# Two attentions in one program: the first 1024 tokens of A transposed on TensorE, output weights through GpSimd's queue, the last 512 queries in two halves

## The chip, the cores and the metric

One core of one Trainium2 chip. The metric is the device time of one execution in microseconds (us), the median of several runs. "Before" is the kernel as it was, "after" the changed one. The span in the trace (first to last traced instruction) is 1.7 to 2.4 us shorter than the time of the same execution; both are named where they matter.

In the lines of the profile TensorE is PE (PEld its weight loads), VectorE DVE, ScalarE ACT, GpSimd POOL, SyncE SP; L752 is line 752 of that kernel. Lines in order of time begin with start in us and duration in us; in brackets is the idle time before it and what ended that. Apart from the 16 heads of attention, "head" is the start of the program. PSUM is the memory that TensorE writes its products to; the program deals it out in banks.

## The reference, cut to what matters

```python
# A: 2048 tokens, D = 448, 16 query heads of 28, ONE key/value head for all
q = (x @ wq).reshape(B, S, 16, 28);  k = x @ wk;  v = x @ wv
p = softmax(q k^T * 28**-0.5)             # full: 16 x 2048 x 2048
a = (p v) @ wo
# B: another x, 16 heads of 28, each position sees 8 earlier ones (steps of 2)
qkv = x @ wqkv
logits = q[s] . k[s - 2*w], w = 0..7      # masked below 0
b = softmax(logits) v[s - 2*w] @ wo
return concatenate([a, b], axis=-1)
```

A has 16 x 2048 x 2048 exponentials. In blocks of 128 keys by 512 queries that is 1024 score blocks. B has few exponentials, and fills gaps on TensorE and VectorE.

## The kernel before

The program is a list of operations, each with an engine, a modelled duration, reads, writes and a priority. A greedy list scheduler inside the program fixes the order on each engine before it is built; the built program has no choice left at run time. The modelled durations and priorities thus decide the order, and only the chip decides the times.

Loads (cut): the first 512 tokens of A come as they are and are transposed on TensorE. The rest come through transposing loads on SyncE's queue (SP). The output weights of A (`wo4`) and B (`wo_B`) come last, on the same queue.

```python
a("act", 0.5, load A_x[0:512] -> xst, W=["xst"], land=3.2, pr=-21)
a("act", 1.1, load wq, first part; gp: the other part)
for c in range(1, NCH):                   # chunks of 512 tokens, NCH = 4
    for t in range(4):
        a("sp", 1.05, transposing load of A_x chunk c -> xT_A, R=["xst"], ...)
for c in range(NCH):
    for t in range(4):
        a("sp", 1.05, transposing load of B_x chunk c -> xT_B, ...)
...
a("sp", 1.5, 4 loads -> wo_B, rel=4);  a("sp", 1.5, 4 loads -> wo4, rel=4)
```

Head: warm-up matmuls, the 16 transposes of chunk 0, K and Q of chunk 0, then the first scores. A further matmul on their squares (`q_sq` for Q, `d_u` for K, with `hq` as weights) completes each of them.

The loop over the score blocks: score slots of three and two PSUM banks in turn (`SLOTS`), one exponential on ScalarE (ACT) for each slot. In the rounds (one slot of three and one of two) that `OFF_AT` names, VectorE (DVE) takes the last bank of a three-bank slot and computes the exponential by a polynomial.

```python
SLOTS = ((0, 1, 2), (3, 4));  PVBANK = 5;  XBANKS = (6, 7);  TAILB = (0, 1, 2, 4);  WARM = 7
OFF_AT = {q: (0, 2, 5, 7) for q in range(1, 16)}            # quad q: 4 heads x 512 queries
OFF_AT.update({q: (0, 2, 3, 5, 7, 8) for q in (5, 9, 13)})
...
for i, (sc, t, tb, j) in enumerate(us):   # scores: 2 or 3 blocks on different row tiles
    matmul(bank(b0 + i), kT[32*j.., 128*tb..], qT[32*j.., sc % 2, t, :], tile_position=(32*j, 0))
a("act", t_exp(w), activation(expT, ps[:, 512*b0 : 512*b0 + w], Exp))
```

The end of a quad (`a_quad_end`): transpose the output product on VectorE, reciprocal, multiply, transpose again, then (every fourth quad) four output blocks through `wo4`. For the last quad this is done in two halves of columns, but both can begin only after the last exponential, since every output product covers all 512 queries.

B's work (`b_all`) is laid in by priorities that grow with `B0 = 22.0` and `BSTEP = 23.6`.

Of the kernel before, what the change touches and what calls it, by code (L numbers as in the profile page):

```python
# [12 lines left out]
D = 448  # L13
H = 16
DH = 28
# [15 lines left out]
TAILB = (0, 1, 2, 4)  # L31
WARM = 7
# [7 lines left out]
OFF_AT.update({q: (0, 2, 3, 5, 7, 8) for q in (5, 9, 13)})  # L40
# [53 lines left out]
class Sched:  # L94
# [49 lines left out]
    def run(self, engines):  # L144
# [44 lines left out]
        while left:  # L189
# [77 lines left out]
            if e == "pe":  # L267
                if o.use is not None and o.use.spare and o.alone and area(T) < (self.WANT if limit is None or T + o.dur + 0.18 <= limit + self.EPS else self.LOW):
                    o.fill = 1
                    o.dur += 0.18  # L270
                    o.dense += 512 - o.use.spare
                elif (o.full and area(T) < (self.FULL[o.full] if T + 0.22 * o.full + 0.2 <= H + self.EPS else self.LOW)
                      and all(d.start is not None and d.end + self.lat(d) <= T for d in o.opt)):
                    o.deps.update(o.opt)
                    o.dur = 0.22 * o.full
                    o.tiled = False
                    o.dense = 512 * o.full
                elif o.fill is not None:
                    o.full = 0
                    o.fill = max(0, min(0 if waiting else 2, round((self.WANT - area(T)) * self.WIN / 512 + 0.3)))  # L280
                    if T > 14 and area(T) > self.LOW:
                        o.fill = max(0, min(o.fill, int((H - 0.12 - self.MODE - T - o.dur + self.EPS) / 0.22)))
                    o.dur += 0.22 * o.fill
                    o.dense += 512 * o.fill
                if o.tiled and not mode:
                    o.dur += self.MODE
                mode = o.tiled
                if o.dense:
                    recent.append((T + o.dur, o.dense))
                    del recent[:-120]  # L290
# [108 lines left out]
class Gen:  # L399
# [63 lines left out]
    def alloc(self, es):  # L463
# [57 lines left out]
        self.xst = self.stage[:, 0:4 * D].rearrange("p (b c) -> p b c", c=D)  # L521
# [63 lines left out]
    def loads(self):  # L585
# [4 lines left out]
        def wload(dst, src, c0, c1):  # L590
# [4 lines left out]
            out=g.xst[:, :, :], in_=g.A_x[0, 0:512, :].rearrange("(b p) c -> p b c", p=128))),  # L595
          W=["xst"], dsem="i_xa0", land=3.2, pr=-21)
# [4 lines left out]
        for c in range(1, NCH):  # L601
            for t in range(4):
                a("sp", 1.05, one(lambda e, c=c, t=t: e.dma_start(
                    out=g.xT_A[:, t, 512 * c:512 * c + 512], in_=g.A_x[0, 512 * c:512 * c + 512, XB0[t]:XB0[t] + 128],
                    transpose=True)), R=["xst"], W=[("xT", c, t)], dsem=f"i_xa{c}.{t}", land=3.8, pr=-20 + c)
        for c in range(NCH):
            for t in range(4):
                a("sp", 1.05, one(lambda e, c=c, t=t: e.dma_start(
                    out=g.xT_B[:, t, 512 * c:512 * c + 512], in_=g.B_x[0, 512 * c:512 * c + 512, XB0[t]:XB0[t] + 128],
                    transpose=True)), W=[("xT_B", c, t)], dsem=f"i_xb{c}.{t}", land=4.5, pr=-16 + c)  # L610
# [8 lines left out]
        a("sp", 1.5, lambda e: [e.dma_start(  # L619
            out=g.wo_B[:, t, :], in_=bass.AP(g.B_wo.tensor, g.B_wo.offset + 7 * t * D, ap=[[D, 7], [DH * D, 16], [1, D]]))  # L620
            for t in range(4)], W=["wo_B"], dsem="i_wob", land=5, pr=2, rel=4, ninc=4)
        a("sp", 1.5, lambda e: [e.dma_start(
# [18 lines left out]
    def a_head(self):  # L641
# [6 lines left out]
        for c in range(NCH):  # L648
            pr = -9 if c == 0 else c
            HB = g.HB if c == 0 else g.LB  # L650
            for kt in range(4 if c == 0 else 0):
                u = Use(f"T{kt}", g.TB[kt:kt + 1])
                for b in range(4):
                    a("pe", 0.1, lambda e, u=u, kt=kt, b=b: e.transpose(  # L654
                        g.psb[:, 1024 * u.bank + 128 * b:1024 * u.bank + 128 * b + 128],
                        g.xst[:, b, XB0[kt]:XB0[kt] + 128], g.ident[:, :]),
                      R=["xst", "ident"], use=u, pr=-16, dense=128)
                dst = g.xT_A[:, kt, 0:512]
                src = lambda u=u: g.psb[:, 1024 * u.bank:1024 * u.bank + 512]
                if kt % 2:  # L660
                    a("dve", 0.42, lambda e, src=src, dst=dst: e.tensor_copy(out=dst, in_=src()), W=[("xT", 0, kt)], use=u, pr=-9)
                else:
                    a("act", t_act(512), lambda e, src=src, dst=dst: e.activation(dst, src(), ACT.Copy),
                      W=[("xT", 0, kt)], use=u, pr=-110)
# [27 lines left out]
            g.a_v(c)  # L692

# [65 lines left out]

    def a_loop(self):  # L760
# [4 lines left out]
        quads = {(sc, t): [[] for _ in range(4)] for sc in range(4) for t in range(4)}  # L765
# [6 lines left out]
        while pos < NU:  # L772
# [9 lines left out]
            def qk(e, us=us, b0=b0, box=[]):  # L782
                for _ in range(box[0].fill):
                    e.matmul(g.bank(b0), g.warm[:, 0:128], g.warm[:, :], start=True, stop=True)
                for i, (sc, t, tb, j) in enumerate(us):
                    if box[0].full:
                        r = e.matmul(g.bank(b0 + i), g.kz[:, j, 128 * tb:128 * tb + 128], g.qT[:, sc % 2, t, :], start=True, stop=True)  # L787
                        continue
                    r = e.matmul(g.bank(b0 + i), g.kT[32 * j:32 * j + 32, 128 * tb:128 * tb + 128],  # L789
                                 g.qT[32 * j:32 * j + 32, sc % 2, t, :], start=True, stop=True, tile_position=(32 * j, 0))  # L790
                return r
            box = []
            o = a("pe", 0.315, lambda e, qk=qk, box=box: qk(e, box=box), R=[("kT", tb // 4) for (_, _, tb, _) in us] + [("qT", sc % 2, t) for (sc, t, _, _) in us],
# [4 lines left out]
            o.opt = {x for (_, _, tb, _) in us for x in g.kz_ops[tb // 4]}  # L798
# [11 lines left out]
            for i in range(na):  # L810
                g.last_exp[b0 + i] = x
                quads[us[i][:2]][us[i][3]].append((us[i], ("expT", n % ERING), g.expT[:, n % ERING, 512 * i:512 * i + 512], 0))
# [5 lines left out]
            while late and late[0][0] <= n // 2:  # L818
                for x in late.pop(0)[1]:
                    qd = x[0][:2]  # L820
# [10 lines left out]
            for u in us:  # L831
                js = quads[u[:2]]
                while all(js):
                    g.pv_group([x.pop(0) for x in js])
                if u[2:] == (15, 3):
# [4 lines left out]
    def pv_group(self, grp):  # L840
        g, a = self, self.s.add
        qd = grp[0][0][:2]
# [3 lines left out]
        def pv(e):  # L846
            for (_, _, tb, j), _, src, w in grp:
                order = [o.seq for o, js in all_pv if j in js]
                first, last = box[0].seq == min(order), box[0].seq == max(order)
                x = e.matmul(g.bank(PVBANK, p0=32 * j, p1=32 * j + 32), g.v_aug[:, w, tb, :], src,  # L850
                             start=first, stop=last, tile_position=(0, 32 * j))
            return x
        o = a("pe", 0.315, pv, R=sorted({y[1] for y in grp}) + sorted(
            {(k, y[3], y[0][2] // 4) for k in ("v_aug", "v_aug1") for y in grp}), pr=-40, dense=700)
# [7 lines left out]
        if g.npv[qd] == 64:  # L862
            g.a_quad_end(*qd)

    def offload(self, n, us):

        g = self
        if n % 2 or us[0][:2] != us[-1][:2]:
            return 0
        if us[0][:2] != g.quad:  # L870
            g.quad, g.round = us[0][:2], n // 2
        return int(n // 2 - g.round in OFF_AT.get(4 * us[0][0] + us[0][1], ()))
# [28 lines left out]
    def a_quad_end(self, sc, t):  # L901
        g, a = self, self.s.add
        end = 12.0 + QT * (4 * sc + t + 1)
        last = sc == 3 and t == 3
        evacs = []
        hv = 2 if last else 1
        for hf in range(hv):
            w, b = 512 // hv, 16 // hv
            cs, bs = slice(w * hf, w * hf + w), slice(b * hf, b * hf + b)
            keys = [hf] if last else [0, 1]  # L910
            kk = lambda n: [(n, t % 2, x) for x in keys]
            p0 = -30 if last else -1
            o = a("dve", t_dve_ps(w), lambda e, cs=cs: e.transpose(out=g.PV_T[:, t % 2, cs], in_=g.bank(PVBANK)[:, cs]),  # L913
                  W=kk("PV"), pr=-30)
            o.deps.update(x for x, _ in g.pvs[sc, t])
            evacs.append(o)
            pt = g.PV_T[:, t % 2, :].rearrange("p (b e) -> p b e", e=32)
            a("dve", 0.25, lambda e, pt=pt, bs=bs: e.reciprocal(out=g.rden[:, t % 2, bs], in_=pt[:, bs, DH]),
              R=kk("PV"), W=kk("rden"), pr=p0)
            a("dve", t_dve_1x(w), lambda e, pt=pt, bs=bs: e.tensor_tensor(  # L920
                out=g.oN[:, bs, :], in0=pt[:, bs, :], in1=g.rden[:, t % 2, bs].unsqueeze(2).to_broadcast([128, b, 32]), op=ALU.mult),
              R=kk("PV") + kk("rden"), W=[("oN", x) for x in keys], pr=p0)
            a("dve", 0.12 + 1.04e-3 * w, lambda e, cs=cs: e.transpose(
                out=g.oTn[:, t, cs], in_=g.oN[:, :, :].rearrange("p b e -> p (b e)")[:, cs]),
              R=[("oN", x) for x in keys], W=[("oTn", t, x) for x in keys], pr=p0)
        g.evacs = evacs
        pr = end + 20
        if t < 3:
            return
        for s4 in range(4):  # L930
            blk = 4 * sc + s4
            if last:
                u = Use(f"F{sc}.{s4}", (TAILB[s4],), late=True)
            else:
                u = Use(f"F{sc}.{s4}", XBANKS)
            for tt in range(4):
                o = a("pe", t_mm(D), lambda e, u=u, s4=s4, tt=tt: e.matmul(  # L937
                    g.bank(u.bank, D), g.oTn[:, tt, 128 * s4:128 * s4 + 128], g.wo4[:, tt, :], start=tt == 0, stop=tt == 3),
                  R=[("oTn", tt, s4 // 2), "wo4"], W=[u], use=u, pr=pr + s4 + tt if not last else -30 + tt, dense=448)
                if last and tt == 0:  # L940
                    o.deps.add(g.last_exp[TAILB[s4]])
# [64 lines left out]
    def b_logits(self, k):  # L1006
# [4 lines left out]
        for t in range(4):  # L1011
# [9 lines left out]
            if k == 0:  # L1021
                op.deps.update(g.s.rd.get("xst", ()))
# [115 lines left out]
```

## Time and profile before

| what | before |
|---|---|
| time, median of 3 (range) | 460.67 us (460.61 to 460.84) |
| span of the profiled run | 459.2 us |
| start to first exponential ("head") | 11.29 us |
| first to last exponential ("stretch") | 440.43 us |
| last exponential to the end ("tail") | 7.47 us |
| blocks on ScalarE / VectorE | 958 / 66 |

The three pieces add up to the span. They come from one trace of each kernel. One more quantity is used, the **excess**: over all exponentials, the time from one start to the next instruction of ScalarE, less 0.8333 ns per column and 60 ns (the densest stretch of before keeps this rule: five exponentials of 13 blocks in 5.85 us). It sums the short stalls behind exponentials; before has 3.97 us. It leaves out the last exponential, and a wait that follows another instruction of ScalarE: 1.47 us in late_tr, 1.14 in old_head and in old_head_66, 1.30 in old_head_hold.

Two lines more of before that are needed later. The first is from the order of events (start in us, duration in us, then engine, line, operation, in brackets the idle time before it and what ended that), the second from the table of transfers, whose last number is the median time from issue to landing:

```profile
8.96 0.39 PE L752 MATMUL ps<-q_sq,hq 128*128 128x512 bf16 x1 [0.26 <-ACT q_sq L744]
...
xT_A<-in_A_x_dram SPq DMA_TRANSPOSE x12, 4.1
```

The matmul on `q_sq` starts as soon as ScalarE has the squares. From it to the first exponential are 11.29 - 8.96 = 2.33 us. A's twelve transposing loads land 4.1 us after their issue, at the median.

### The profile page before, as it was taken

To read this page: it belongs to the slowest core of one execution; us is meant where nothing else is said; L and a number is where in the kernel's file an instruction comes from. 1 tells how busy PE (TensorE), PEld (TensorE's weight loads), DVE (VectorE), ACT (ScalarE), POOL (GpSimd) and SP (SyncE) were. 2 spreads that over 40 slices of the span, in tenths; PEclk is the share of its full clock that TensorE was granted. 3 is DMA by queue.
4 is the path that set the end of the run, shared out by engine and by line. 5 is a ranking of instruction groups with operands and counts; after the bars stand their busy time and mean duration, and the time that the engine had idled before them with its cause. 6 is when DMAs were issued, how large, how long until landed. Compare 5 with 4: busy or idle time off the path is not lost.

```text
span 459.2 us, 8717 instructions
## 1 busy us (share of the span) xinstructions
PE 427.7 (93%) x3682; PEld 163.6 (36%) x3682; DVE 380.7 (83%) x622; ACT 444.9 (97%) x430; POOL 9.4 (2%) x29
## 2 busy tenths in 40 slices
PE   8999999999999989999899999899899998989997
PEld 3333232323533324234353342224244342325343
DVE  6556889988798898989688889998988969889883
ACT  3999999999999999999999999999999999999994
POOL 7000000000000000000000000000000000000000
PEclk9999999999999999999999999999999999999999
DMA  7774303002201002020220120002022221214001
GB/s 152 128 162 95 109 27 100 1 1 90 92 15 40 19 10 82 20 81 22 81 91 30 44 83 18 0 13 92 0 97 92 70 78 30 72 31 142 10 1 61
DMA packets 42102, 27.34 MB, mean 60 GB/s; under 512 B 17474, under 2 KB 41904, under 8 KB 42064
## 3 DMA queue, kind: packets, MB, share of 16 engines
q1 hardware_dynamic: 40464, 25.28, 19.6%
q0 software_dynamic: 304, 0.73, 0.6%
q10 hardware_dynamic: 1296, 0.79, 0.5%
q8 instruction: 29, 0.48, 0.4%
q14 instruction: 9, 0.07, 0.1%
HBM read 17.60 MB, written 5.52 MB: 50 GB/s over the span
## 4 chain that ended last, share of the span: by engine, by line
ACT 86%; PE 11%; DVE 1%; DMA 1%; issue 0%
ACT expT L806 85%; PE ps L789 2%; PE ps L1079 2%; PE ps L850 2%; PE ps L787 1%; DMA stage<-in_A_x_dram 1%; PE ps L978 1%; PE ps L1086 1%; PE ps L937 1%; ACT e_t L1054 0%; PE ps L654 0%; PE ps L738 0%; PE ps L1028 0%; PE ps L434 0%; PE ps L993 0%
## 5 line engine op out<-in xcount | busy, mean ns | idle before, releaser
L806 ACT ACTIVATE expT<-ps 128x1024 bf16<-128x1024 f32 (+1 forms) x410 | 438.8, 1209 | 2.1 <-PE ps L789 1.9
L789 PE MATMUL ps<-qT,kT 32*128 32x512 bf16 x824 | 122.3, 385 | 11.6 <-ACT expT L806 9.3
L850 PE MATMUL ps<-expT,v_aug 128*32 128x512 bf16 x958 | 94.8, 389 | 1.0 <-ACT expT L806 1.0
L787 PE MATMUL ps<-qT,kz 128*128 128x512 bf16 x200 | 59.6, 383 | 9.9 <-ACT expT L806 9.4
L789 PEld LDWEIGHTS ps<-qT,kT 32*128 32x128 bf16 x824 | 30.1, 91 | 91.7 <-ACT expT L806 68.4
L883 DVE TENSOR_SCALAR d_x<-ps 128x512 f32<-128x512 f32 x66 | 45.4, 688 | 17.9 <-PE ps L789 16.8
L850 PEld LDWEIGHTS ps<-expT,v_aug 128*32 128x32 bf16 x958 | 24.3, 93 | 62.0 <-issue 55.4
L1073 DVE TENSOR_TENSOR prod<-Vsh,a_n 128x896 bf16<-128x896 bf16 x64 | 37.5, 614 | 7.9 <-PE ps L1079 7.9
L1019 DVE TENSOR_TENSOR stage<-qTB,kTB 112x1024 bf16<-112x1024 bf16 x64 | 42.3, 674 | 1.8 <-PE ps L1028 1.7
L1079 PE MATMUL ps<-ident,prod 128*112 128x128 bf16 x512 | 41.8, 224 | 0.0
L894 DVE SCALAR_TENSOR_TENSOR d_u<-d_u,d_x 128x1024 f32<-128x1024 f32 x33 | 40.1, 1215 | 0.1
L896 DVE SCALAR_TENSOR_TENSOR dexp<-d_u,d_x 128x1024 int16<-128x1024 f32 x33 | 40.0, 1213 | 0.1
L892 DVE SCALAR_TENSOR_TENSOR d_u<-d_x 128x1024 f32<-128x1024 uint16 x33 | 39.9, 1209 | 0.2
L1079 PEld LDWEIGHTS ps<-ident,prod 128*112 128x112 bf16 x512 | 34.2, 130 | 14.7 <-issue 10.9
L978 PE MATMUL ps<-xT_B,wqkv 128*128 128x512 bf16 x128 | 38.9, 383 | 0.0
L787 PEld LDWEIGHTS ps<-qT,kz 128*128 128x128 bf16 x200 | 12.2, 97 | 31.1 <-ACT expT L806 28.9
L1028 PEld LDWEIGHTS ps<-ones,stage 112*128 112x128 bf16 x512 | 18.5, 96 | 7.8 <-issue 4.8
L1028 PE MATMUL ps<-ones,stage 112*128 112x4 bf16 x512 | 21.2, 167 | 0.0
L738 PE MATMUL ps<-xT_A,wq 128*128 128x512 bf16 x64 | 19.8, 384 | 0.1
L1086 PE MATMUL ps<-wo_B,oT 112*128 112x448 bf16 x64 | 18.1, 357 | 0.0
L993 PE MATMUL ps<-wqv,xT_B 128*128 128x448 bf16 x64 | 17.5, 356 | 0.0
L913 DVE STREAM_TRANSPOSE PV_T<-ps 128x512 f32<-128x512 f32 (+1 forms) x17 | 11.4, 676 | 6.7 <-PE ps L850 6.5
(103 smaller groups left out, 303.3 us busy)
## 6 DMA issues: line engine op xcount, KB each, us to landing
Vsh<-v_scratch SPq DMA_DIRECT2D x16, 896.0 KB, 4.6
v_scratch<-Vst SPq DMA_DIRECT2D x16, 112.0 KB, 1.7
out_dram<-outB SPq DMA_DIRECT2D x16, 112.0 KB, 1.7
out_dram<-outA SPq DMA_DIRECT2D x14, 112.0 KB, 1.7
wqkv<-in_B_wqkv_dram SPq DMA_DIRECT2D x1, 672.0 KB, 5.4
stage<-in_A_x_dram ACTq DMA_DIRECT2D x1, 448.0 KB, 4.0
wo_B<-in_B_wo_dram SPq DMA_DIRECT2D x4, 98.0 KB
wo<-in_A_wo_dram SPq DMA_DIRECT2D x4, 98.0 KB
```

The costliest lines, as they stand in the source:

```text
L787: r = e.matmul(g.bank(b0 + i), g.kz[:, j, 128 * tb:128 * tb + 128], g.qT[:, sc % 2, t, :], start=True, stop=True)
L789: r = e.matmul(g.bank(b0 + i), g.kT[32 * j:32 * j + 32, 128 * tb:128 * tb + 128], g.qT[32 * j:32 * j + 32, sc % 2, t, :], start=True, stop ...
L806: x = a("act", t_exp(w), lambda e, b0=b0, w=w, n=n: e.activation(g.expT[:, n % ERING, 0:w], g.ps[:, 512 * b0:512 * b0 + w], ACT.Exp, scale ...
L850: x = e.matmul(g.bank(PVBANK, p0=32 * j, p1=32 * j + 32), g.v_aug[:, w, tb, :], src, start=first, stop=last, tile_position=(0, 32 * j))
L883: o = a("dve", t_dve_ps(512), lambda e: e.tensor_scalar(out=xx[:, 512 * h:512 * h + 512], in0=g.bank(bank), scalar1=-128.0 * A2, scalar2=1 ...
L892: a("dve", t_dve_1x(1024), lambda e: e.scalar_tensor_tensor(out=u, in0=lo, scalar=EP * F, in1=lo, op0=ALU.add, op1=ALU.mult), R=di, W=["d_ ...
L894: a("dve", t_dve_1x(1024), lambda e: e.scalar_tensor_tensor(out=v, in0=u, scalar=EQ * F * F, in1=lo, op0=ALU.add, op1=ALU.mult), R=["d_u"] ...
L896: a("dve", t_dve_1x(1024), lambda e: e.scalar_tensor_tensor(out=out, in0=v, scalar=EL / F ** 3, in1=xx, op0=ALU.mult, op1=ALU.subtract), R ...
L978: a("pe", t_mm(512), lambda e, u=u, t=t, kt=kt, w=w: e.matmul(g.bank(u.bank), g.wqkv[:, kt, w * D + KC * t:w * D + KC * t + 128], g.xT_B[: ...
L1019: op = a("dve", t_dve_2x(1024), lambda e, t=t, qv=qv, kv=kv: e.tensor_tensor(out=g.prodT[0:KC, t, :, :], in0=qv, in1=kv, op=ALU.mult), R=R ...
L1028: r = e.matmul(g.bank(u.bank, 128).rearrange("p (h w) -> p h w", w=WIN)[:, 4 * t:4 * t + 4, w], g.prodT[0:KC, t, w, :], g.ones4[:, :], sta ...
L1079: a("pe", 0.056, lambda e, u=u, t=t, w=w: e.matmul(g.bank(u.bank, 128, 128 * t, p1=KC), g.prod2[:, w, KC * t:KC * t + KC], g.ident[:, :], ...
```

## The change

Its intent: a shorter tail, because the last 512 queries are done as two halves of 256, of which the first is finished before the last exponential; a second chunk of tokens that does not need the transposing loads; SyncE's queue relieved, so that B starts earlier; and a little less exponential work on VectorE, 62 blocks for 66.

The diff, cut to its core (left out: a modelled cost in the scheduler, by which scores that follow filling matmuls now take longer in its plan):

```diff
-TAILB = (0, 1, 2, 4)
-WARM = 7
+TAILB = (4, 0)
+WARM = 9
-OFF_AT.update({q: (0, 2, 3, 5, 7, 8) for q in (5, 9, 13)})
+OFF_AT.update({q: (0, 2, 3, 5, 7, 8) for q in (7,)})
+OFF_AT[15] = (0, 2, 3, 5)                       # and only in its first half
 # loads
+a("act", 0.5, load A_x[512:1024] -> xst[:, 4:8], W=[("xst", 1)], land=4.5, pr=-19)
-for c in range(1, NCH):   a("sp", 1.05, transposing loads of A, R=["xst"])
+for c in range(2, NCH):   a("sp", 1.3,  transposing loads of A, R=[("xst", 0)])
-                          a("sp", 1.05, transposing loads of B)
+                          a("sp", 1.3,  transposing loads of B)
-a("sp", 1.5, wo_B);  a("sp", 1.5, wo4)
+a("gp", 4, wo_B);    a("gp", 4, wo4)
 # head
-if c == 0: transposes on TensorE
+if c < 2:  g.a_tr(c)                             # chunk 1 too: two banks, four DVE copies
 # last quad
+def parts(self, u):                              # one block = two key blocks x 256 queries
+    if u[:2] == (3, 3):
+        return [(2 * (u[2] % 8) + i, 256 * (u[2] // 8), 256) for i in range(2)]
+    return [(u[2], 0, 512)]
-for i, (sc, t, tb, j) in enumerate(us): one matmul of 512
+for i, u in enumerate(us):
+    for k, (tb, q0, nq) in enumerate(g.parts(u)): one matmul of nq columns
-if g.npv[qd] == 64: a_quad_end(sc, t)            # both halves at the end
+if g.npv[qd] == (64 if len(qd) == 2 else 32): a_quad_end(sc, t[, half])
```

## The prediction

> **What bounds the kernel now.** I read the page's busy shares first, then who makes ScalarE wait, then the chain that ended last, then the first 12 and the last 20 us in order of time. ScalarE (ACT) is busy 97% of the span, and the chain goes through it:
>
> ```profile
> PE 427.7 (93%) x3682; PEld 163.6 (36%) x3682; DVE 380.7 (83%) x622; ACT 444.9 (97%) x430; POOL 9.4 (2%) x29
> ACT 86%; PE 11%; DVE 1%; DMA 1%; issue 0%
> ACT outA L944 <- PE ps L937: 3.4, 1, 3.4
> ACT expT L806 <- PE ps L789: 1.9, 1, 1.9
> ```
>
> Those two waits stand at the two ends: 1.9 us before the first exponential, 3.4 us after the last. Between them no wait is charged to ACT. So the time is three pieces: a head until the first exponential at 11.29, a stretch of exponentials until 434.81 + 16.91 = 451.72, and a tail until 459.2, that is 7.48 us. The stretch is 440.43 us. The groups by shape give what it is made of:
>
> ```profile
> L806 ACT ACTIVATE expT<-ps 128x1024 bf16<-128x1024 f32 x270 | 269.7, 1066 | 0.1
> L806 ACT ACTIVATE expT<-ps 128x1536 bf16<-128x1536 f32 x139 | 207.2, 1490 | 2.0 <-PE ps L789 1.9
> L806 ACT ACTIVATE expT<-ps 128x512 bf16<-128x512 f32 x1 | 0.8, 761 | 0.0
> L883 DVE TENSOR_SCALAR d_x<-ps 128x512 f32<-128x512 f32 x66 | 45.4, 688 | 17.9 <-PE ps L789 16.8
> ```
>
> There are 1024 score blocks of 128x512. VectorE (DVE) does 66 of them (L883), ACT the other 958 = 2x270 + 3x139 + 1. One block costs ACT 1490 - 1066 = 0.424 us; the number of instructions (410, two for every five blocks) does not depend on who does the block.
>
> The head, in order of time: load, transposes, K and Q, first exponential.
>
> ```profile
> 0.81 4.02 DMA stage<-in_A_x_dram
> 4.88 1.89 PE ps L654 x16
> 8.31 0.60 ACT q_sq L744
> 10.14 0.67 DVE kT L684
> 11.29 5.97 ACT expT L806 x5
> ```
>
> The tail, the same way (VectorE, then the last issue of SyncE):
>
> ```profile
> 452.41 0.78 DVE L913 STREAM_TRANSPOSE PV_T<-ps 128x256 f32<-128x256 f32 x2 [5.22 <-PE ps L850]
> 453.99 0.76 DVE L923 STREAM_TRANSPOSE oTn<-oN 128x256 bf16<-128x256 bf16 x2
> 454.67 0.65 DVE L1082 CAST oT<-ps 112x512 bf16<-112x512 f32 x1
> 455.25 1.14 DVE L947 CAST outA<-ps 128x448 bf16<-128x448 f32 x2
> 456.35 0.62 DVE L1089 CAST outB<-ps 128x448 bf16<-128x448 f32 x1
> 457.00 0.33 SPq L1091 DMA_DIRECT2D out_dram<-outB  x1
> ```
>
> The tail is not A's alone: B's last block (L1082, L1089) sits between A's steps on DVE, and its store is the last one issued.
>
> **What the Trainium skill says.** "ScalarE: Activation LUTs", What ACT_TABLE_LOAD costs, gives 186 ns + 0.833 ns per column for an ACTIVATE with immediates, and an overlap of about 93 ns back to back. That is 1039 ns for 1024 columns and 1466 for 1536; the trace has 1066 and 1490, within 3%, and its 0.424 us for 512 columns is the 0.427 of the page. "TensorE: Matmul & The Clock Gate", Part 1, gives 426.7 ns for 512 columns while PE is cold, 215.7 when warm, and about 3.4 us of activity in a free-running window to get there. The trace agrees on the pitches: seven warm-up matmuls take 3.17 us, sixteen transposes 1.89 (0.107 apart, so still cold), the four Q matmuls at 7.24 take 1.03, so warm. "TensorEngine Tiling (Array Packing)", Key Properties, lets different tiles work in parallel; the three scores of L789 take 0.39 us together, as much as one alone (mean 385 ns). "DMA: Bandwidth & Descriptors", Issuing engines are not separate DMA queues, says that another issuer only saves the sequencer's time; that is SyncE's 3.37 + 1.79 us for wo_B and wo at 41 to 46 us here.
>
> **The change part by part.**
>
> Fewer blocks on DVE. Before: twelve quads with 4 and three (5, 9, 13) with 6, 48 + 18 = 66. After: thirteen of quads 1 to 14 with 4, quad 7 with 6, and quad 15 with 4 in its first half only: 52 + 6 + 4 = 62. ACT gets four blocks back: 4 x 0.424 = +1.70 us, all on the path, since ACT has no idle time to take them. DVE loses 4 x 0.688 + 2 x (1.209 + 1.215 + 1.213) = 10.0 us, on an engine that doesn't bound.
>
> Stalls between exponentials. The densest stretch, 11.29 to 17.14, has five for 13 blocks in 5.85 us: 13 x 0.427 + 5 x 0.06. By that rule 958 blocks and 410 instructions take 433.4 us; eight L1054 cost some 0.31 each (89.06 to 89.37) and four gcol 0.06, 436.1 in all. The stretch is 440.4, so some 4 us are short stalls, mostly (my reading) where DVE must empty a third bank. Four of 66 such rounds fewer: -0.25.
>
> Last quad in halves. Each score is now two matmuls of 256 columns, issued one after the other on the same row tile before the next tile's, so three blocks take four steps of 0.107 us instead of two: about 0.21 us longer. After the exponential of a three-bank slot ACT has 0.91 us of the other slot to cover a 0.39 us score group; at 0.6 us this still fits if PE is prompt, and PE is not always. I put +0.3 over the 13 rounds. The output product alternates over four tiles, so its length stays 0.39.
>
> Head. The first 512 tokens take the same path as before. A second 448 KB load is put on ACT's queue behind the first and behind wq, so the first should land near 4.83. Nine warm-up matmuls instead of seven end near 1.25 + 9 x 0.427 = 5.1 instead of 4.2, 0.2 us after that landing; against it, the clock may be granted earlier. The second chunk's 16 transposes and four copies (4 x 0.42 us of DVE) must fit the idle gaps between 8.3 and 10.8; a copy ahead of L756 would cost up to 0.4. I put +0.2. SyncE sends 8 transposing loads of A (1.26 us each) instead of 12, so wqkv goes out 5 us earlier than 22.5 and B starts earlier. That doesn't move the stretch: in the head ACT shows no wait for keys even now. B's loads carried no hold on x in the diff's old side either; they only stand behind fewer of A's.
>
> GpSimd issues wo_B and wo: eight issues of 0.55 to 0.9 us, about 6 us from 10.2, done before its first v_aug copy at 17.4. Off the path: 0.
>
> Tail. From the last exponential to PV_T stays 0.69. With one half left, the VectorE chain is 0.43 + 0.18 + 0.40 + 0.42 (256-column means of L913, L918, L920, L923) and three hand-overs of 0.06 = 1.61, against 454.48 - 452.41 = 2.07. Then a matmul 0.06 + 0.2 later for the second block, its result 0.39 on, an ACT copy of 0.54 and a hand-over of 0.03; the store and the closing barrier, 459.2 - 457.0 = 2.2. Sum: 0.69 + 1.61 + 0.26 + 0.39 + 0.57 + 2.2 = 5.7 against 7.48, so -1.75. It needs B's last block out of the way: B starts 5 us earlier and DVE has 10 us less, so it should be done near 445.
>
> Sum: +1.70 - 0.25 + 0.3 + 0.2 - 1.75 = +0.2.
>
> **The rivals.** First, the tail gains nothing, because B's last block still ends last or the second half's output products wait for the first half (they share one bank, and the first half's DVE exponentials are ready late). For: in the trace B's blocks run some 40 us behind the times that the code sets. Against: DVE is busy only 6.4 of the last 11.7 us before the last exponential. Then about 462.5. Second, the halves or the head cost more: score groups late in each of 13 rounds by 0.2, or PE waiting in order for the second load before K and Q. For: PE is 93% busy. Against: PE waits for ACT 97 us in 242 waits. Then 463 to 464. Third, a better gain: the warm clock comes before the transposes (16 at 0.056 instead of 0.107, limited by the copies to some 0.5 us), and lighter quads 5, 9 and 13 remove more stalls than counted, 1 us. Then 458.5.
>
> **Range and chances.** +0.2 gives 460.9; I shade it to 460.6, since less on DVE and an earlier B can only shorten stalls. The range 458.4 to 463.0 holds the tail gain from none to full and either head. A change of 2% is 9.2 us, more than head stalls and tail together could lose without a new wait inside the stretch: 0.96 within, 0.02 each side.
>
> **What would show it.** L883 x62, ACT with 143 instructions of 1536 columns and 266 of 1024, and a stretch 1.3 to 2 us longer; the first exponential between 10.9 and 11.8; last exponential to end 5.5 to 6.2 us, with no L1089 after L947 and a store of A as the last one. Wrong would be: new waits of ACT for L789 or its successor inside the stretch, a first exponential after 12, a B store last, or a stretch not longer at all (then the stalls went with the four blocks).

## The result, and the profile after

| what | before | after |
|---|---|---|
| time, median (range, runs) | 460.71 us (460.58 to 461.08, 6) | 460.76 us (460.52 to 462.23, 6) |
| span of the profiled run | 459.2 | 458.8 |
| head | 11.29 | 12.02 |
| stretch | 440.43 | 441.01 |
| tail | 7.47 | 5.76 |
| blocks on ScalarE / VectorE | 958 / 66 | 962 / 62 |
| excess | 3.97 | 3.03 |

The ratio of the times is 1.0006, with a 95% interval of 0.9993 to 1.002: the same. A ratio here is always the mean time of one kernel's fast runs over that of the other's of the same rounds, so it is not quite the ratio of the medians that are quoted.

The page of after, its busy line and its chain of work that ended last:

```profile
PE 427.7 (93%) x3818; PEld 165.8 (36%) x3818; DVE 373.9 (81%) x617; ACT 445.3 (97%) x429; POOL 14.6 (3%) x37
...
ACT 93%; PE 4%; DMA 1%; DVE 1%; ACTq 0%; issue 0%
```

ScalarE's waits in after (total us, times, longest), the two that count:

```profile
ACT outA L968 <- PE ps L961: 2.8, 1, 2.8
ACT expT L832 <- PE ps L815: 2.2, 1, 2.2
```

ScalarE still bounds. Its two long waits are still only those at the ends: the tail's is shorter (2.8 for 3.4), the head's longer (2.2 for 1.9). VectorE has become less busy and TensorE is unchanged.

The groups by shape (count, then busy us and mean ns of one, then idle time before them):

```profile
L832 ACT ACTIVATE expT<-ps 128x1024 bf16<-128x1024 f32 x266 | 267.7, 1077 | 0.1
L832 ACT ACTIVATE expT<-ps 128x1536 bf16<-128x1536 f32 x143 | 214.0, 1497 | 2.2 <-PE ps L815 2.2
...
L911 DVE TENSOR_SCALAR d_x<-ps 128x512 f32<-128x512 f32 x62 | 42.6, 687 | 20.3 <-PE ps L815 19.4 <-PE ps L812 0.6
```

The counts are those that were predicted: 143, 266 and 62.

The head of after in order of time (TensorE, and the first exponential on ScalarE):

```profile
7.48 1.04 PE L751 MATMUL ps<-xT_A,wq 128*128 128x512 bf16 x4 [0.36 <-DVE wq L636]
9.47 0.40 PE L693 MATMUL ps<-ident,stage 128*128 128x128 bf16 x4 [0.31 <-DMA stage<-in_A_x_dram]
9.71 0.38 PE L765 MATMUL ps<-q_sq,hq 128*128 128x512 bf16 x1
12.03 1.45 ACT L832 ACTIVATE expT<-ps 128x1536 bf16<-128x1536 f32 x1 [2.23 <-PE ps L815]
```

L693 is a transpose of the second chunk. TensorE stood at it until the second load had landed, and the `q_sq` matmul (L765, L752 of before) had to wait behind it, although its squares were ready at 9.15 (8.55 + 0.60). It starts at 9.71 instead of 8.96. From it to the first exponential is 2.32 us, as before. So all of the +0.73 in the head passes through this one place in TensorE's order. A part of it is older: Q (L751) begins at 7.48 instead of 7.24, since VectorE's copy of wq began at 7.11 instead of 6.48. That leaves some 0.5 us for the wait behind the transposes. Two of the nine warm-up matmuls of the program came to stand behind the first sixteen transposes (at 6.30 and 6.73), so the first transposes began at 4.87, as before (4.88).

The tail of after (TensorE, VectorE, ScalarE and the two issuing queues, in order of time):

```profile
448.49 4.55 ACT L832 ACTIVATE expT<-ps 128x1536 bf16<-128x1536 f32 x4
...
453.54 0.45 DVE L938 STREAM_TRANSPOSE PV_T<-ps 128x256 f32<-128x256 f32 x1 [5.45 <-PE ps L878]
...
454.72 0.45 DVE L947 STREAM_TRANSPOSE oTn<-oN 128x256 bf16<-128x256 bf16 x1
...
455.23 0.55 PE L961 MATMUL ps<-wo,oTn 128*128 128x448 bf16 x2 [1.44 <-DVE oTn L947]
455.63 0.62 DVE L971 CAST outA<-ps 128x448 bf16<-128x448 f32 x1 [0.46 <-PE ps L961]
455.82 0.54 ACT L968 ACTIVATE outA<-ps 128x448 bf16<-128x448 f32 x1 [2.78 <-PE ps L961]
...
456.39 0.36 ACTq L973 DMA_DIRECT2D out_dram<-outA  x1
```

One half's chain, no work of B in it, and a store of A is the last one. B's last cast had been at 430.06 (456.35 before), although B had not started earlier: its first matmul on the tokens begins at 38.6 us (38.0 before).

The halves hardly slowed the score groups. Six matmuls of 256 columns take as long as three of 512 (0.39 us before). The ends of matmuls are modelled in a trace, but the semaphores agree: a group of six tells ScalarE 0.434 us after its first start, a group of three 0.415.

```profile
428.94 0.40 PE L815 MATMUL ps<-qT,kT 32*128 32x256 bf16 x6
```

Where the time went, in spans: head +0.73, stretch +0.58, tail -1.71, in all -0.40. The stretch is +1.71 for four more blocks (4 x 0.427), -0.94 of excess, and -0.17 in the last exponential, which the excess leaves out. Outside the span after takes 2.04 to 2.13 us in all its six runs, before 1.71 to 1.81 in most of its runs (and 2.2 to 2.35 in some): about +0.35. This cancels the -0.40 nearly.

### The profile page after: what moved, and what is told of

The parts are those of the page before. It is cut to its first block, busy times and chain, and to the rows that moved or that the text cites. A ratio compares the mean times of both kernels' runs of the same rounds, so it can differ in the third digit from the quotient of the medians.

```text
span 458.8 us, 8985 instructions
## 1 busy us (share of the span) xinstructions
PE 427.7 (93%) x3818; PEld 165.8 (36%) x3818; DVE 373.9 (81%) x617; ACT 445.3 (97%) x429; POOL 14.6 (3%) x37
## 4 chain that ended last, share of the span: by engine, by line
ACT 93%; PE 4%; DMA 1%; DVE 1%; ACTq 0%; issue 0%
ACT expT L832 92%; DMA stage<-in_A_x_dram 1%; PE ps L1103 1%; PE ps L815 1%; PE ps L812 1%; PE ps L878 1%; ACT e_t L1078 1%; PE ps L961 0%; ACTq L594 0%; PE ps L1052 0%; DVE qT L769 0%; DVE kT L676 0%; ACTq L593 0%; ACT outA L968 0%; ACTq L595 0%
## 5 line engine op out<-in xcount | busy, mean ns | idle before, releaser
L815 PE MATMUL ps<-qT,kT 32*128 32x512 bf16 (+1 forms) x859 | 120.8, 373 | 10.9 <-ACT expT L832 8.2
L878 PE MATMUL ps<-expT,v_aug 128*32 128x512 bf16 (+1 forms) x1022 | 95.2, 376 | 0.2 <-ACT expT L832 0.2
L812 PE MATMUL ps<-qT,kz 128*128 128x512 bf16 (+1 forms) x229 | 62.0, 363 | 9.6 <-ACT expT L832 9.1
L911 DVE TENSOR_SCALAR d_x<-ps 128x512 f32<-128x512 f32 x62 | 42.6, 687 | 20.3 <-PE ps L815 19.4
L1103 PE MATMUL ps<-ident,prod 128*112 128x128 bf16 x512 | 43.5, 224 | 0.1
L922 DVE SCALAR_TENSOR_TENSOR d_u<-d_u,d_x 128x1024 f32<-128x1024 f32 x31 | 37.6, 1214 | 0.2
L924 DVE SCALAR_TENSOR_TENSOR dexp<-d_u,d_x 128x1024 int16<-128x1024 f32 x31 | 37.6, 1213 | 0.1
L920 DVE SCALAR_TENSOR_TENSOR d_u<-d_x 128x1024 f32<-128x1024 uint16 x31 | 37.5, 1210 | 0.1
L812 PEld LDWEIGHTS ps<-qT,kz 128*128 128x128 bf16 x229 | 15.0, 97 | 29.5 <-ACT expT L832 27.4
L751 PE MATMUL ps<-xT_A,wq 128*128 128x512 bf16 x64 | 20.0, 384 | 0.7 <-DVE wq L636 0.4
L961 PE MATMUL ps<-wo,oTn 128*128 128x448 bf16 x64 | 16.8, 356 | 1.4 <-DVE oTn L947 1.4
```

The costliest lines, as they stand in the source:

```text
L812: r = e.matmul(g.bank(b0 + i, nq, nq * k), g.kz[:, j, 128 * tb:128 * tb + 128], g.qT[:, sc % 2, t, q0:q0 + nq], start=True, stop=True)
L815: r = e.matmul(g.bank(b0 + i, nq, nq * k), g.kT[32 * j:32 * j + 32, 128 * tb:128 * tb + 128], g.qT[32 * j:32 * j + 32, sc % 2, t, q0:q0 + ...
L878: x = e.matmul(g.bank(PVBANK, nq, q0, p0=32 * j, p1=32 * j + 32), g.v_aug[:, w, tb, :], src[:, nq * k:nq * k + nq], start=first, stop=last ...
L911: o = a("dve", t_dve_ps(512), lambda e: e.tensor_scalar(out=xx[:, 512 * h:512 * h + 512], in0=g.bank(bank), scalar1=-128.0 * A2, scalar2=1 ...
L920: a("dve", t_dve_1x(1024), lambda e: e.scalar_tensor_tensor(out=u, in0=lo, scalar=EP * F, in1=lo, op0=ALU.add, op1=ALU.mult), R=di, W=["d_ ...
L922: a("dve", t_dve_1x(1024), lambda e: e.scalar_tensor_tensor(out=v, in0=u, scalar=EQ * F * F, in1=lo, op0=ALU.add, op1=ALU.mult), R=["d_u"] ...
```

## The experiments

Twelve kernels ran. In the table, ratio is to the kernel before in the same rounds; before had medians of 460.89, 460.59, 460.85 and 461.0 us in the four batches (first four, next four, next three, last).

Each edit makes the scheduler lay a new order on all engines, so a run changes more on the chip than its edit says. And the first exponential moves from trace to trace, with the landing of the loads: 10.63 to 11.40 us in the nine traces with the old head, 11.47 to 12.63 in the four with the new one (late_tr apart).

| run | median us (range, runs) | ratio [95%] | head | stretch | tail | excess | ACT/DVE blocks |
|---|---|---|---|---|---|---|---|
| blocks66 | 462.37 (461.9 to 463.31, 6) | 1.0029 [1.0014, 1.0044] | 12.63 | 439.98 | 7.82 | 3.60 | 958/66 |
| late_tr | 462.10 (461.61 to 462.38, 6) | 1.0019 [1.0005, 1.0033] | 11.22 | 442.55 | 5.77 | 3.07 | 962/62 |
| old_head | 465.45 (463.52 to 468.64, 6) | 1.0095 [1.0065, 1.0125] | 10.96 | 447.29 | 5.78 | 8.22 | 962/62 |
| old_head_66 | 465.34 (464.68 to 467.71, 6) | 1.0103 [1.0078, 1.0128] | 10.63 | 444.26 | 8.50 | 6.65 | 958/66 |
| tail_only62 | 460.29 (460.14 to 461.33, 5) | 0.9996 [0.9983, 1.0008] | 10.92 | 441.35 | 5.96 | 3.17 | 962/62 |
| tail_only66 | 462.87 (462.53 to 462.95, 4) | 1.0045 [1.003, 1.006] | 11.40 | 440.18 | 9.33 | 3.62 | 958/66 |
| old_head_hold | 463.25 (463.04 to 464.84, 4) | 1.0063 [1.0049, 1.0078] | 10.96 | 444.95 | 6.97 | 5.62 | 962/62 |
| after_sp | 461.13 (461.03 to 461.46, 4) | 1.0011 [0.9997, 1.0025] | 11.64 | 441.51 | 5.96 | 3.13 | 962/62 |
| gp_only | 463.43 (462.33 to 463.92, 4) | 1.0046 [1.0031, 1.0061] | 11.16 | 443.44 | 7.47 | 7.16 | 958/66 |
| early66 | 458.25 (458.04 to 458.55, 5) | 0.9943 [0.9931, 0.9956] | 10.92 | 439.38 | 6.31 | 2.86 | 958/66 |
| mix64 | 458.64 (458.33 to 459.58, 5) | 0.9953 [0.9941, 0.9966] | 10.99 | 439.77 | 5.94 | 2.55 | 960/64 |
| early66_new_head | 461.67 (461.63 to 461.67, 5) | 1.0015 [1.0001, 1.0028] | 11.47 | 439.51 | 8.62 | 3.05 | 958/66 |

### What the four blocks bought: blocks66

```diff
 # after, but
-OFF_AT.update({q: (0, 2, 3, 5, 7, 8) for q in (7,)})
+OFF_AT.update({q: (0, 2, 3, 5, 7, 8) for q in (5, 9, 13)})
```

> The changed kernel with six DVE blocks in quads 5, 9 and 13 again and four in quad 7, so 66 DVE blocks instead of 62. Theory (a block costs ACT 0.427 us and brings back some 0.06 to 0.25 us of stalls): stretch 441.0 - 1.7 + 0.6 = 439.9 or less, time 459.7 or less. Rival (the three heavy quads are what stalled ACT before: excess over the dense rule was 4.0 us before and 3.0 after): stretch 440.7 to 441, excess back to 4, time 460.4 to 460.8.

Measured: 462.37 us, later than either expectation. The stretch fell by 1.03 us, but the tail grew by 2.06 (and the head by 0.60, since its loads landed later). The end of blocks66 in order of time:

```profile
455.75 0.69 DVE L1106 CAST oT<-ps 112x512 bf16<-112x512 f32 x1 [0.35 <-PE ps L1103]
456.36 1.15 DVE L971 CAST outA<-ps 128x448 bf16<-128x448 f32 x2
...
457.65 0.62 DVE L1113 CAST outB<-ps 128x448 bf16<-128x448 f32 x1
458.30 0.33 SPq L1115 DMA_DIRECT2D out_dram<-outB  x1
```

B's last block (L1106, L1113) is back in the tail and its store is the last one issued, as in the kernel before. With this head and these places the short tail came only with the four blocks taken from VectorE; the +1.71 and the -1.71 of the change then belong together. Whether the amount of work or its order decides is tested further below.

### What the head cost: late_tr

```diff
 # after, but the second chunk's transposes come after the first scores
-  W=[("xst", 1)], dsem="i_xa1", land=4.5, pr=-19)
+  W=[("xst", 1)], dsem="i_xa1", land=8.5, pr=-19)
```

The number is the modelled landing time. It changes no transfer, only the place of the transposes in TensorE's order.

> The changed kernel, but the schedule takes the second load of x to land 8.5 us after issue instead of 4.5, so that its 16 transposes stand behind the first scores in PE's order and no longer before L765. Theory (PE stood still for that load with the q_sq matmul behind it): the matmul after q_sq starts at 9.2 instead of 9.71, first exponential near 11.5 instead of 12.02, time near 460.3. Rival (L765 is late because Q was late, wq having landed later): first exponential 11.9 to 12.1, time unchanged at 460.8.

Measured: the head fell to 11.22, and another wait took its place. From the order of events of late_tr:

```profile
8.89 0.39 PE L765 MATMUL ps<-q_sq,hq 128*128 128x512 bf16 x1
...
11.32 0.95 PE L693 MATMUL ps<-ident,stage 128*128 128x128 bf16 x14
...
19.65 2.37 ACT L832 ACTIVATE expT<-ps 128x1536 bf16<-128x1536 f32 x2 [1.47 <-PE ps L815]
```

L765 does not wait for the load any more: it starts 1.72 us after Q (7.17), as in before, where after took 2.23. So the wait of some 0.5 us is shown. But now the keys of the second chunk come late, and ScalarE stalls 1.47 us before the exponential at 19.65. The median rose to 462.10 (against before the intervals of late_tr and after overlap). So the early place costs about 0.5 us and the late one about 1.5.

The rest of the +0.73 is Q's later start, and this goes with the second load too, but late_tr does not test it: the last part of wq that Q needs landed between 6.21 and 6.51 us in the nine traces without this load, and between 6.49 and 7.69 in the five with it (7.09 in after, 6.76 in late_tr).

In after, after_sp, blocks66 and early66_new_head the first transpose of the second chunk starts at 9.47, 9.08, 10.08 and 8.93 us, and the first exponential 2.56, 2.55, 2.55 and 2.54 later. (In the last of these the trace shows no wait for the load any more, but Q began only at 7.41, so TensorE itself was that late.)

### The old head under the new loads: old_head, old_head_66, old_head_hold, gp_only

```diff
 # after, but only the first 512 tokens are transposed on TensorE
-WARM = 9
+WARM = 7
-a("act", 0.5, load A_x[512:1024] -> xst[:, 4:8], ...)
-for c in range(2, NCH): transposing loads of A
+for c in range(1, NCH): transposing loads of A
-if c < 2: g.a_tr(c)
+if c < 1: g.a_tr(c)
```

> The changed kernel with the head of before: only 512 tokens transposed on PE, no second early load of x, seven warm-up matmuls; the rest as changed. Theory (head, stretch and tail add up, and the new head lost 0.73 us): first exponential near 11.3 instead of 12.02, stretch of exponentials as in the changed kernel (441.0, within 0.5), tail 5.8, time near 460.0. Rival (the later first exponential was paid back inside the stretch by an earlier B and by keys that are ready sooner): first exponential 11.3 but the stretch 441.6 or more, time 460.6 to 461.

old_head_66 is the same with the edit of blocks66 as well:

> Old head and 66 DVE blocks together, with the new tail. If the parts add up: first exponential 11.3, stretch 439.5 to 440.4, tail 5.8; span 457 to 457.5, time 458.6 to 459.3. If the stalls of the heavy quads eat the blocks: stretch 441, time 460.

Measured: both near 465.4, more than 4 us over every expectation. The head is short, but ScalarE stalls after it. The waits of old_head (us in total, times, longest):

```profile
ACT expT L829 <- PE ps L812: 5.8, 3, 2.3
...
PEld ps L656 <- DMA xT_A<-in_A_x_dram: 3.4, 3, 1.9
```

L656 is a matmul for keys. The transposing loads of A land a median of 6.3 us after issue (4.1 before), and TensorE waits for them. The rounds of old_head_66 say the same with 66 blocks (2.1 us stalled at 16.6, 1.1 at 20.9, 1.1 at 29.4). The suspicion fell on the output weights: GpSimd issues them between 10.4 and 15.2 us, just when these loads are under way. Two runs tested it. First old_head_hold, where GpSimd's issues wait until the last chunk's keys are there (they went out from 32.2 us on); for this the two lines also move behind the head in the program:

```diff
 # old_head, but
-a("gp", 4, wo_B, rel=4);                    a("gp", 4, wo4, rel=4)
+a("gp", 4, wo_B, R=[("kT", 3)], rel=4);     a("gp", 4, wo4, R=[("kT", 3)], rel=4)
```

> The run old_head (old head, wo from GpSimd, 62 blocks, new tail) with wo's loads made to wait for A's last keys, so they start near 27 us and not at 10. Theory (the early wo loads delay A's transposing loads): the transposing loads of A land in a median near 4.1 us and not 6.3, no stall over 0.3 us before 35, first exponential 11.0 to 11.3, time 460.0 to 460.5 against 465.4. Rival (another order of work or the clock made old_head stall): 464 or more again.

Measured: the loads land in 3.7 us again, but the time is 463.25 and ScalarE still stalls, 2.65 us before the exponential at 20.57 and 1.30 us before the one at 30.16. So the weights are not the whole story of old_head. Nor is the 2.2 us between the two medians the weights' alone: the two runs of old_head with a mean clock of 0.999 took 463.52 and 463.99, the four with 0.997 and less up to 468.64. (In the trace of old_head_hold the granted clock was also at half between 453.3 and 456.7, beside a tail of 6.97 where old_head has 5.78.) Then gp_only, the kernel before with nothing changed but the issuer of these weights:

```diff
 # before, but
-a("sp", 1.5, wo_B);  a("sp", 1.5, wo4)
+a("gp", 4, wo_B);    a("gp", 4, wo4)
```

> The kernel before, with one difference: the output weights wo_B and wo are issued by GpSimd (from some 10 us) rather than by SyncE after the transposing loads. Head, tail and 66 blocks as before. Theory (early weights delay the transposing loads, and the old head needs these for its second chunk of keys): A's transposing loads land with a median near 6 us rather than 4.1, ScalarE stalls for 2 to 5 us in sum between 15 and 32 us, stretch 442.5 to 445, time 463 to 465.5. Rival (the stall of old_head came from the order in which SyncE's slower modelled issues put the second chunk's work on TensorE, and the early weights cost nothing by themselves): no stall over 0.3 us before 32 us, stretch 440 to 441, time 460.6 to 461.2. In between (stall of about 1.5 to 2 us, 462 to 462.5) both have a part.

Measured: 463.43 us, ratio 1.0046. The waits of gp_only:

```profile
ACT expT L806 <- PE ps L789: 4.8, 3, 2.1
PEld ps L667 <- DMA xT_A<-in_A_x_dram: 2.9, 2, 2.7
```

and from its table of transfers:

```profile
xT_A<-in_A_x_dram SPq DMA_TRANSPOSE x12, 6.5
```

The key matmuls of the second chunk, first in before, then in gp_only with the exponential that waited:

```profile
14.15 0.81 PE L667 MATMUL ps<-xT_A,wk 128*128 128x512 bf16 x3
...
14.03 0.59 PE L667 MATMUL ps<-xT_A,wk 128*128 128x512 bf16 x2
16.85 0.39 PE L667 MATMUL ps<-xT_A,wk 128*128 128x512 bf16 x1 [2.22 <-DMA xT_A<-in_A_x_dram]
17.98 1.45 ACT L806 ACTIVATE expT<-ps 128x1536 bf16<-128x1536 f32 x1 [2.09 <-PE ps L789]
```

4.1 became 6.5 us, TensorE waits up to 2.7 us for one of these loads, and ScalarE stalls 2.1 and 0.8 us after the head. The fourth load of the second chunk, issued at 9.8 us in both, landed at 14.1 in before and at 16.8 here, and the last key matmul, which needs it, starts at 14.59 and at 16.85. So giving the weights to another issuer costs the old kernel 2.6 us (by the medians; 2.1 by the ratio). The theory holds here, the rival (nothing by itself) falls: the scheduler laid another order here too (TensorE's differs from the 44th matmul on), but the key matmuls stand at the same place, and the load came late. A part of it comes by way of the clock: the trace has it at half between 17.1 and 20.5, right after TensorE's wait, and the one run with a mean clock of 1.0 took 462.33 where the three with 0.996 took 463.3 to 463.9. (old_head has such a lapse from 25.3 to 28.7.) In after the loads are as late (median 6.1), but the second chunk of keys no longer depends on them (the third chunk's loads had landed by 15.5, its key matmuls begin at 17.75), and no single stall over 0.37 us is left. The second chunk on TensorE is what makes the early weights harmless.

For old_head_hold something else remains. It models SyncE's transposing loads at 1.3 us each, where before has 1.05, and this puts the second chunk's work later in TensorE's order: the key matmuls stand at 15.4 to 17.4 us. tail_only62 below has 1.05 and no such stall. No run changed this number alone, so this part is argued and not shown.

### The tail alone: tail_only62, tail_only66

```diff
 # old_head, and
-for ...: a("sp", 1.3, transposing loads of A and of B)
+for ...: a("sp", 1.05, transposing loads of A and of B)
-a("gp", 4, wo_B);    a("gp", 4, wo4)
+a("sp", 1.5, wo_B);  a("sp", 1.5, wo4)
```

> Head and all loads as in the kernel before (wo from SyncE at 41 us, seven warm-ups, 12 transposing loads of A), but the last quad in halves and 62 DVE blocks. Theory (wo moved to 10 us is what made the old head stall; without it the parts add up): first exponential 11.3, no stall over 0.25 us before 35 us, stretch 440.43 + 1.71 - 1.0 = 441.1 (excess near 3), tail 5.8; span 458.2, time 459.9 to 460.0 (span + 1.75). Rival (the old head stalls with any new order of the schedule, wo or not): stalls of 2 us or more between 15 and 32 us, time 463 or more.

tail_only66 is this with the edit of blocks66:

> As tail_only62 but with 66 DVE blocks (six in quads 5, 9, 13). In the run blocks66 the tail came to 7.8 us because B's last block stood in it. Theory (it is the blocks taken from DVE that bought the short tail): stretch 439.5 to 440.0, but B's last cast and store are in the tail, which is 7.2 to 8.0; time 460.3 to 461. Rival (halves alone shorten the tail): tail 5.8, time 458.5.

Measured: 460.29 us with 62 blocks, stretch 441.35, tail 5.96, no stall over 0.31 us. Its interval contains 1, so against before it is the same. Its median is 0.47 under after's, but of other rounds, and the two intervals against before overlap. With 66 blocks at the old places: 462.87 us, the tail 9.33, with B's last cast at 458.14 and its store at 458.79, long after the last exponential (451.6). That is more than expected (tail 7.2 to 8.0, time up to 461). So with the six-block quads at 5, 9 and 13 the halves are worse than nothing, whichever the head.

### The issuer under the new head: after_sp

```diff
 # after, but
-a("gp", 4, wo_B);    a("gp", 4, wo4)
+a("sp", 1.5, wo_B);  a("sp", 1.5, wo4)
```

> The changed kernel with wo issued by SyncE again, behind B's transposing loads. Theory: with chunk 1 already transposed on PE the early wo cost nothing that ACT waits for, so first exponential 12.0 (varies by 0.6 with the landing of wq), stretch 440.5 to 441.3, tail 5.8; but the time outside the span, 2.1 us with eight more GpSimd loads and 1.75 before, goes back to 1.75, so time 460.2 to 460.5. Rival (the 0.35 us outside the span comes from elsewhere): time 460.8.

Measured: the loads of A land in a median of 3.9 us again, those of wqkv in 5.1 instead of 8.2, but the time is 461.13, interval 0.9997 to 1.0025. So with the new head nothing is gained by giving the weights back. And the time outside the span stayed at 2.06 to 2.13 us: the early weights are not what made it longer, as I had thought possible. By the other runs it goes with the code: 1.72 to 1.82 with everything old but the issuer (gp_only), 1.89 to 2.05 with the old head and the new tail (seven kernels), 2.02 to 2.14 with the new head as well. So roughly 0.2 comes with the tail and 0.1 with the head. What it is made of no trace shows, since it lies outside.

### Where VectorE's blocks stand: early66, mix64, early66_new_head

The tail needs B out of the way. Is it the amount of work on VectorE that decides, or where it stands?

```diff
 # tail_only62, but (early66)
-OFF_AT.update({q: (0, 2, 3, 5, 7, 8) for q in (7,)})
+OFF_AT.update({q: (0, 2, 3, 5, 7, 8) for q in (1, 3, 14)})
```

> The old head with the tail in halves (tail_only62), but with 66 VectorE blocks, the six-block quads moved to 1, 3 and 14, away from 5, 9 and 13. Theory (what put B's last block into the tail of tail_only66 and blocks66 is where VectorE's work stands, not only its amount): B's last block is out before the last exponential, tail 5.8 to 6.8, stretch 439.7 to 440.4 (four blocks fewer for ScalarE at 0.427, against about 0.9 of more short stalls), time 459.0 to 459.8, that is some 1.0 to 1.5 us below before. Rival (66 blocks are too much for VectorE wherever they stand): B's last cast and store in the tail, tail 8 to 9.5, time 462 to 463.

```diff
 # tail_only62, but (mix64)
-OFF_AT.update({q: (0, 2, 3, 5, 7, 8) for q in (7,)})
+OFF_AT.update({q: (0, 2, 3, 5, 7, 8) for q in (8, 12)})
-B0 = 22.0;  BSTEP = 23.6
+B0 = 25.0;  BSTEP = 22.5
```

> tail_only62 with 64 VectorE blocks (six-block quads 8 and 12) and B's times set to start at 25.0 with a step of 22.5 rather than 22.0 and 23.6, so that B ends earlier. Theory (two blocks fewer for ScalarE are worth 0.85 less some 0.45 of stalls, and B still ends before the tail): stretch 440.4 to 441.1, tail 5.8 to 6.2, time 459.2 to 460.0. Rival (B's earlier steps take VectorE from the exponentials): stalls grow, stretch 441.5 or more, time 460.3 or more; or B's last block falls into the tail, time 461 or more.

Measured: 458.25 and 458.64 us, both better than before and after (ratios 0.9943 and 0.9953; within 2%, but both intervals lie below 1, and below that of after). They came out better than I had expected. early66 has as many blocks on VectorE as before, and a tail of 6.31:

```profile
451.88 0.62 DVE L1110 CAST outB<-ps 128x448 bf16<-128x448 f32 x1
452.41 0.43 DVE L944 STREAM_TRANSPOSE oTn<-oN 128x256 bf16<-128x256 bf16 x1
...
454.07 0.36 ACTq L970 DMA_DIRECT2D out_dram<-outA  x1
```

B's last cast falls between two steps of A's last half and delays it by about half a microsecond, but A's store is the last one. So the rival, that 66 blocks are too many wherever they stand, is wrong. Also the excess is 2.86 with 66 blocks and 3.17 with 62: the number of VectorE's blocks alone does not set the short stalls.

Does the place 1, 3, 14 work by itself? The last run puts it under the new head:

```diff
 # after, but (early66_new_head)
-OFF_AT.update({q: (0, 2, 3, 5, 7, 8) for q in (7,)})
+OFF_AT.update({q: (0, 2, 3, 5, 7, 8) for q in (1, 3, 14)})
```

> The changed kernel with one difference: 66 VectorE blocks again, the six-block quads in 1, 3 and 14 (where early66 had its short tail) instead of quad 7 alone. Theory (the place of the six-block quads decides whether B's last block is out in time): tail 5.8 to 6.8, stretch some 1.7 shorter than the changed kernel's 441.0, so 459.1 to 459.9. Rival (no rule of place: the greedy order in which the program lays B's remaining work after a different head decides, and it lays B's last cast here behind the last exponential): B's last cast and store after the last exponential, tail 7.5 to 9.5, first exponential 12 to 12.7, time 462 to 464.

Measured: 461.67 us, tail 8.62.

```profile
456.06 0.63 DVE L1113 CAST outB<-ps 128x448 bf16<-128x448 f32 x1 [0.49 <-PE ps L1110]
456.82 0.62 DVE L971 CAST outA<-ps 128x448 bf16<-128x448 f32 x1
```

B's last cast now comes in the midst of A's last outputs. The theory of place falls, and its rival came true: the same three quads are good under one head and bad under the other. What decides is the position of B's last block in the order that the greedy scheduler makes, and this jumps with small edits anywhere. early66 and mix64 are placements that were tried and that the chip confirmed, not the result of a rule; mix64 moves B's times as well, and no run separates the two.

## Why the prediction was right, and where only its sum was

The prediction was 460.6 us in a range of 458.4 to 463.0, with 0.96 for within 2%; the time was 460.76. Its sum of +0.2 us stands beside a measured +0.05 (-0.40 in the span, +0.35 outside). Term by term:

| term | predicted | measured | shown by |
|---|---|---|---|
| four blocks more on ScalarE | +1.70 | +1.71 by 4 x 0.427 | counts; the stretch of early66 is 1.97 below tail_only62, excess included |
| stalls | -0.25 | -0.94, and -0.17 in the last exponential | excess 3.97 to 3.03 |
| halves in the score groups | +0.3 | about 0 | six matmuls in 0.40 us, three in 0.39; by the semaphores 0.434 and 0.415 |
| head | +0.2 | +0.73 | L765 at 9.71 for 8.96; late_tr |
| GpSimd issues the weights | 0 | 0 in this kernel, +2.6 on the kernel before | after_sp, gp_only |
| tail | -1.75 | -1.71 | 5.76 for 7.47; blocks66 |
| outside the span | not in the sum | about +0.35 | all runs of after |

**Right with their mechanism.** The counts, the worth of a block and the chain of the tail (inside it two misses cancel: 0.50 us and not 0.69 from the last exponential to the first transpose, 2.4 and not 2.2 after the last store's issue). The tail's condition was named too: B's last block must be out of the way. The reason given for it is not borne out: B did not start 5 us earlier (38.6 for 38.0), and its last cast came at 430 and not near 445. Blocks66 shows what happens otherwise, and the first rival was thus a real danger; only its time, 462.5, belongs to a kernel with 66 blocks (462.37).

**Mis-sized: the head.** The prediction said that the second chunk's transposes "must fit the idle gaps". It asked whether the time was there, not whether TensorE, which keeps its order, would stand at the first of them until the second load landed. That was its second rival, "PE waiting in order for the second load before K and Q", and it came true at one matmul, for some 0.5 us, and 0.73 with the later wq. The reason that the sum did give, nine warm-up matmuls that end 0.2 us after the first load, did not come true: two of them stand behind the transposes.

**Two of its own signs failed.** The first exponential came at 12.03, where after 12 was to be "wrong", and the stretch grew by 0.58 and not by 1.3 to 2 us. The one is the head, the other the stalls and the halves.

**Mis-sized: the halves.** "Three blocks take four steps of 0.107 us instead of two" is refuted: of the six matmuls of a group three start within 14 ns and the other three about 0.12 us after the first, so the two matmuls of one row tile did not hold back the other tiles.

**Mis-sized: the stalls, and their cause.** The prediction put them down to rounds in which VectorE empties a third bank, so to the number of blocks. The number alone does not set them, by one trace each: at 66 blocks the excess is 3.6 with the quads 5, 9 and 13 (blocks66, tail_only66), and 2.86 and 3.05 with 1, 3 and 14. The third rival, "lighter quads 5, 9 and 13 remove more stalls than counted", was nearer. Why before has 0.35 more than tail_only66 stays open.

**Right for another reason: GpSimd.** "Off the path: 0" looked at GpSimd's own time. The transfers that it starts early are not free: they made A's loads land 2.2 us later in after (6.1 for the 3.9 of after_sp) and 2.4 us later in gp_only. It was 0 here because the second chunk had been taken off these loads by another part of the change.

**Compensation.** The stalls and the halves came out 1.0 to 1.2 us better than predicted, the head and the outside about 0.9 worse. The total was met by this, and the wide range allowed for it.

**Open.** The +0.35 outside the span. The spread of after's runs: its two slow ones (462.23 and 461.41) had mean granted clocks of 0.993 and 0.997, but no trace was taken in one of them. (In the traced run, with 0.998, the clock is at half only from 456.6 on, after the last matmul, where it costs nothing.) The part of old_head's stall that comes from the order.

## What to carry to other kernels

When work moves to another engine or queue, look at what it now runs beside: the weights cost their new issuer nothing and made the transfers beside them land some 2 us later, and a transpose put into an idle gap made the matmul behind it wait some 0.5 us for its load. A change with several parts can be a bargain in which a part looks pointless alone (with the other quads in place, four blocks for a short tail; a second chunk on TensorE that makes early weights harmless), so test the parts in combination and not only one by one. With a greedy schedule, a tail that depends on whether the other job is finished is worth a search over placements, but every find must be run on the chip, and the one that was tried under another head did not carry over.

## What the Trainium skill lacked or had wrong

- "DMA: Bandwidth & Descriptors", Issuing engines are not separate DMA queues: it says that all issuers' transfers run on the same DMA engines and interleave, and that another issuer only saves the sequencer's time. The first half fits what was seen here, but the section gives no number for it. Eight loads of 98 KB issued from 10.4 to 15.2 us raised the median landing of the transposing loads from 4.1 to 6.5 us (gp_only), and the time by 2.6 us. Another issuer also changed when the transfers start, and that cost more than SyncE's 5 us of issuing were worth (after_sp: nothing).
- "TensorEngine Tiling (Array Packing)", Key Properties: it says that tiles work independently, but the page says nothing of several matmuls in a row on one tile. Six of 256 columns, two on each of three tiles and written tile by tile, took 0.40 us, three of 512 took 0.39.
- "TensorE: Matmul & The Clock Gate", Part 4: it gives about 275 ns for a 128x128 transpose in one kernel, and not how closely they follow each other. Here one takes 311 ns before the full clock and 219 with it, and in a row they start every 107 ns and every 56 ns. It also says that the full clock does not engage for transposes. In after it was granted at 6.0 us, in the midst of sixteen of them, and the last of these already start 56 ns apart, so they do run at it; warm-up matmuls stood before, so this does not show whether transposes count towards it.
- No page tells why the device time outside the traced span differs between two such programs: 1.7 to 1.8 us in most runs of before (2.2 to 2.4 in the others), 2.0 to 2.1 in all of after.
